# GEGLU feed-forward on one core: the head's transposing transfers of x move to ScalarE's queue in halves

## The chip, the cores and the metric

The kernel runs on one core of a Trainium2 chip. The metric is device time in microseconds (us), the median of three runs. The engines are called by the profile's short names: PE (TensorE matmul), PEld (TensorE weight load), DVE (VectorE), ACT (ScalarE), POOL (GpSimd), SP (SyncE). SP and ACT can each start DMA transfers on a queue of their own; "SPq" and "ACTq" are the times in which these two engines issue. A "transposing transfer" is a DMA that reads rows of x from DRAM and writes them transposed into SBUF.

## The reference

```python
B, S, D, F = 32, 32, 1024, 3584          # x is (1024 tokens) x 1024, bf16

def reference(x, w_gate, w_up, w_down):
    return (_gelu(x @ w_gate) * (x @ w_up)) @ w_down     # gelu: tanh approximation
```

The kernel does both big products by a scheme of Strassen's kind with seven products of half-size blocks. In the first stage x transposed is cut into four blocks of 512 model dimensions by 512 tokens, and the two weight matrices are treated as the other operand: for one 128-column strip of F, `a11` and `a12` are the upper and lower half of w_gate's rows, `a21` and `a22` those of w_up. `b11`, `b12` are the upper half of the model dimension for tokens 0 to 511 and 512 to 1023, `b21`, `b22` the lower half for the same tokens. Sums of weights (`s1` to `s4`) and of x blocks (`t1` to `t4`) enter the seven products.

## The kernel before

The work around the change is the head, the first 30 us. Its instructions are written out by hand in the order in which each engine is to run them (`tc.manual_schedule()`); a semaphore is put wherever one instruction needs another's result. Each engine runs its own list in order, so an instruction that waits holds everything behind it on that engine.

Every DMA signals its end on one of eight completion semaphores. They are given out in turn, and a DMA that comes eighth after another has to wait until that other one has landed before it is issued. The built instruction lists show these waits.

The head goes like this:

- The product `a12 b21` needs no sums, so it is computed ahead for 24 strips of 128 columns, in six groups of four (`group_ahead` and the loops before it, lines 326 to 340, 344 and 352). One strip is four matmuls (`k` = 0 to 3, one for each 128 rows of `b21`) into one bank of PSUM. Then ACT or DVE copies the bank to SBUF (`ahead`, lines 299 and 338), in groups 0 to 3 by turns (strips 0 and 2 of a group on ACT, 1 and 3 on DVE), in groups 4 and 5 on ACT alone.
- There are eight banks: six with the tag "A" and two with the tag "C", each handed out in turn. A strip can begin only when the copy that empties its bank has run. Groups use the tags CCAA, AAAA, CCAA, AAAA, AACC, CCAA.
- The first two 128-row pieces of `b21` don't come from a transposing transfer: the rows of x are loaded as they are (`x_nat`, two transfers, `load_nat`), transposed on PE through an identity matrix (line 264) and copied by DVE (line 267). The other two pieces, and the whole of `b11`, `b12` and `b22`, come by transposing transfers (`load_xT`, line 218): one of 256 KB for the rest of `b21`, and one of 512 KB each for the others, all four issued by SP.
- The columns of w_gate for the groups ahead come in `a12a` (groups 0 and 1) and `a12b` (groups 2 to 5) by `load_ahead` (line 211), the weights of the first chunks in `wu` and `wg` by `load_w` (line 135), nearly all issued by SP.
- DVE forms `t1 = b12 - b11` (line 345) and `t2 = b22 - t1` (351) between the adds of the first products (303), then `t3`, `s3` and `t4`; POOL forms the sums `s1`, `s2`, `s4` of chunk 0 from `wu`, `wg` and `a12a` as they land.
- ACT's list begins with three DMA issues: `probe` (line 207), a fetch of 128 bytes of w_gate that nothing reads, the second half of `x_nat`, and the first half of `a12a` of group 1. Then come the load of the activation table and the copies.

After the head the kernel loops over chunks of two strips, PE-bound, and then computes the second product from the stored gelu products.

Of the kernel before, what the change touches and what calls it, by code (L numbers as in the profile page):

```python
# [13 lines left out]
def kernel(  # L14
# [20 lines left out]
    nc = tc.nc  # L35
    P = nc.NUM_PARTITIONS
    fp32 = mybir.dt.float32
    f32r = mybir.dt.float32r
    bf16 = mybir.dt.bfloat16
# [9 lines left out]
    DT, FT = D // P, F // P  # L49
    KD = DT // 2  # L50
# [4 lines left out]
    KQ = DT // 4  # L55
# [8 lines left out]
    wg_r = w_gate.rearrange("(dt dp) f -> dp dt f", dp=P)  # L64
# [8 lines left out]
    xpool = one.enter_context(tc.tile_pool(name="x", bufs=1))  # L73
# [33 lines left out]
    def acc(tag):  # L107
        return ps1.tile([P, NB], fp32, name=f"ps{tag}", tag=tag, bufs=BANKS[tag])
# [28 lines left out]
    def load_w_all(ci, which):  # L137

        alloc_w(ci, which)
        if (ci, which) != (NCH - 1, 0):  # L140
            load_w(nc.sync, ci, which, 0, KD if which == 0 and a12_stays(ci) else DT)
            return


        for d0 in (0, KD):
            load_w(nc.sync, ci, which, d0, d0 + KD)
# [4 lines left out]
    def quads(ci, fl=None):  # L151
        cols = slice(None) if fl is None else slice(fl * P, (fl + 1) * P)
        wg, wu = w_tiles[ci, 0], w_tiles[ci, 1]
        a12 = wg[:, KD:, cols]
        if a12_stays(ci):
            i, j = divmod(chunks[ci][0], KB)
            a12 = a12_ahead[i][:, :, j * P : (j + FC) * P][:, :, cols]
        return wg[:, :KD, cols], a12, wu[:, :KD, cols], wu[:, KD:, cols]
# [3 lines left out]
    def sums(ci, *engs):  # L162

        a11, a12, a21, a22 = quads(ci)
        s1, s2, s4, s3 = (
            spool.tile([P, KD, FC * P], f32r, name=n, tag=n)[:, :, : len(chunks[ci]) * P]
            for n in ("s1", "s2", "s4", "s3")
        )
        s_tiles[ci] = (s1, s2, s3, s4)
        yield engs[0].tensor_tensor(s1, a21, a22, ADD)  # L170
        yield engs[1].tensor_tensor(s2, s1, a11, SUB)  # L171
        yield engs[2].tensor_tensor(s4, a12, s2, SUB)  # L172
        yield engs[3].tensor_tensor(s3, a11, a21, SUB)  # L173
# [17 lines left out]
    NB_P = NB // P  # L191
# [3 lines left out]
    with tc.manual_schedule():  # L195
        def load_nat(eng, dt, p0, p1):
            eng.dma_start(  # L197
                out=x_nat[:, p0:p1, dt * P : (dt + 1) * P],
                in_=xf[p0 * P : p1 * P, (KD + dt) * P : (KD + dt + 1) * P].rearrange("(b p) d -> p b d", p=P),
            )  # L200
# [1 line left out]
        assert KQ == 2  # L202
        load_nat(nc.sync, 0, 0, NB_P)


        probe = xpool.tile([P // 8, KQ, 2], bf16, name="probe")
        nc.scalar.dma_start(out=probe, in_=wg_r[::8, KD : KD + KQ, :2])

        def load_ahead(i, k0, k1, eng=nc.sync):
            f0 = i * KB  # L210
            eng.dma_start(
                out=a12_ahead[i][:, k0:k1, :],
                in_=wg_r[:, KD + k0 : KD + k1, f0 * P : (f0 + KB) * P],
            )

        def load_xT(nb, d0, d1):
            t = ((b11, b12), (b21, b22))[d0 // KD][nb]
            nc.sync.dma_start_transpose(
                out=t[:, d0 % KD : (d1 - 1) % KD + 1, :], in_=xf[nb * NB : (nb + 1) * NB, d0 * P : d1 * P]
            )  # L220

        load_ahead(0, 0, 1)
        load_nat(nc.scalar, 1, 0, NB_P)
        load_ahead(0, 1, 2)
        load_xT(0, KD + KQ, DT)
        load_ahead(1, 0, KQ, nc.scalar)
        a12_ahead += [spool.tile([P, KD, KB * P], bf16, name="a12b", tag=t) for t in ("s2", "s4", "s1", "s3")]
        for i in (0, 1):
            load_ahead(i, KQ, KD)
        def load_halves(i):  # L230
            for k in range(0, KD, KQ):
                load_ahead(i, k, k + KQ)

        load_halves(2)
        load_halves(3)
        for which in (1, 0):
            load_w_all(0, which)
        load_ahead(4, 0, KD)
        load_xT(0, 0, KD)
        load_xT(1, 0, KD)  # L240
        load_ahead(5, 0, KD)
        load_xT(1, KD, DT)
        for which in (1, 0):
            load_w_all(1, which)

        def gelu(src, tag, bufs):
            h = ework.tile([P, NB], bf16, name=tag, tag=tag, bufs=bufs)[:, : src.shape[-1]]
            nc.scalar.activation(h, src, ACT.Gelu_apprx_tanh)  # L248
            return h


        gelu(ident[:, :1], "h0", 6)

        warm_ps = acc("A")
        for _ in range(NWARM):
# [26 lines left out]
        def product_ahead(ps, i, j, k0=0, k1=KD, cols=slice(None)):  # L282
            for k in range(k0, k1):
                nc.tensor.matmul(  # L284
                    ps[:, cols],
                    lhsT=a12_ahead[i][:, k, j * P : (j + 1) * P],
                    rhs=b21[:, k, cols],
                    start=(k == 0 and not cols.start),
                    stop=(k == KD - 1),
                    skip_group_check=True,  # L290
                )

        def group_ahead(i, tags, copies=(nc.scalar.copy,), between=None):
            for j, tag in enumerate(tags):
                if between and 2 * j == KB:
                    between()
                ps = acc(tag)
                product_ahead(ps, i, j)
                copies[j % len(copies)](ahead_at[i * KB + j], ps)
# [35 lines left out]
        for i in (0, 1):  # L335
            for j in range(KB):
                product_ahead(ps[i][j], i, j, KQ)
                both[j % 2](ahead_at[i * KB + j], ps[i][j])
        group_ahead(2, "CCAA", both)
        group_ahead(3, "AAAA", both)  # L340
        chunk0 = sums(0, *[nc.gpsimd] * 3, nc.vector)
        for _ in range(3):
            next(chunk0)
# [275 lines left out]
```

## Time and profile before

| | us |
|---|---|
| time, median of 3 runs (lowest to highest) | 274.18 (273.29 to 275.09) |
| profiled execution: first to last instruction (span) | 272.0 |
| PE busy in it | 267.1 (98%) |
| DVE, ACT, POOL busy | 201.2, 116.1, 119.3 |
| first matmul of the groups ahead starts | 4.31 |
| first matmul that reads the transposed half of `b21` | 8.89 |
| SP's issues of the four transposing transfers | 1.34, 5.32, 1.67, 3.65 |

The profiled execution's own time is known only as its span; the median of the runs is 2.2 us above it, for what lies before the first and after the last instruction and for differences between executions.

How to read it: a timeline row gives the start, the length, the engine, the line, and the operation as output <- input, and in brackets how long the engine sat idle before it and what ended that. A DMA row on SPq or ACTq is the issue alone; how long a transfer takes to land is told in the DMA view, counted from the start of the issue. Buffer numbers are left out of names, so `b` stands for any of the four blocks and `t` for any of their sums.

### The profile page before, as it was taken

How to read it: one execution, taken by the hardware profiler on the slowest of the kernel's cores; microseconds unless marked ns; L12 is line 12 of the kernel's file. 1: busy time of each engine (PE TensorE's matmuls, PEld its weight loads, DVE VectorE, ACT ScalarE, POOL GpSimd, SP SyncE). 2: the span in 40 equal slices, each digit the busy share in tenths (PEclk: the TensorE clock that was granted, in tenths of full speed). 3: DMA queues.
4: the chain of work that ended last, by engine and by line, in shares of the span. 5: the costliest groups of instructions: out<-in, count | busy, mean ns of one | idle time of the engine just before them, and what ended most of it. 6: DMA issues, size and time to landing. Idle time of an engine off the chain costs nothing.

```text
span 272.0 us, 3399 instructions
## 1 busy us (share of the span) xinstructions
PE 267.1 (98%) x1199; PEld 193.4 (71%) x1212; DVE 201.2 (74%) x205; ACT 116.1 (43%) x189; POOL 119.3 (44%) x60
## 2 busy tenths in 40 slices
PE   8999999999999999999999999999999999999995
PEld 4444776886787688688688687764458888888884
DVE  1448998886976876876787458569999999997721
ACT  2335865545644643645636535434000307770000
POOL 1090099976995994994995978000000000000000
PEclk9999999999999999999999999999999999999999
DMA  7999130504505505415234290005981437855111
GB/s 174 323 227 281 39 99 17 158 25 130 154 2 154 154 4 154 128 27 157 69 88 118 50 319 17 0 2 182 356 273 60 158 112 253 276 187 174 54 61 58
DMA packets 56048, 35.86 MB, mean 132 GB/s; under 512 B 9824, under 2 KB 56032, under 8 KB 56032
## 3 DMA queue, kind: packets, MB, share of 16 engines
q1 hardware_dynamic: 52736, 33.17, 42.6%
q10 hardware_dynamic: 3296, 2.49, 2.9%
q8 instruction: 9, 0.15, 0.2%
q14 instruction: 7, 0.06, 0.1%
HBM read 31.72 MB, written 2.10 MB: 124 GB/s over the span
## 4 chain that ended last, share of the span: by engine, by line
PE 97%; DMA 1%; issue 0%; SPq 0%; DVE 0%
PE psA L273 38%; PE psA L425 24%; PE psC L273 19%; PE psC L425 7%; PE psA L284 5%; PE psC L284 3%; PE psC L588 1%; DMA a12a<-in_w_gate_dram 1%; SPq L197 0%; PE tp L264 0%; DVE o_last L589 0%
## 5 line engine op out<-in xcount | busy, mean ns | idle before, releaser
L273 PE MATMUL psA<-t,s 128*128 128x512 f32 x224 | 57.2, 397 | 0.0
L248 ACT ACTIVATE h<-c 128x512 bf16<-128x512 f32 x56 | 34.6, 631 | 41.6 <-DVE c L303 41.6
L273 PEld LDWEIGHTS psA<-t,s 128*128 128x128 f32 x224 | 42.1, 188 | 9.5
L170 POOL TENSOR_TENSOR s<-wu 128x1024 fp32r<-128x1024 bf16 x13 | 28.8, 2215 | 32.9 <-DMA wu<-in_w_up_dram 27.9
L171 POOL TENSOR_TENSOR s<-s,wg 128x1024 fp32r<-128x1024 f32 x14 | 31.7, 2263 | 15.0 <-DVE s L170 14.0
L173 POOL TENSOR_TENSOR s<-wg,wu 128x1024 fp32r<-128x1024 bf16 x13 | 28.4, 2188 | 0.0
L273 PE MATMUL psA<-b,wg 128*128 128x512 bf16 x119 | 27.8, 379 | 0.6
L273 PE MATMUL psA<-t,a22r 128*128 128x512 f32 x112 | 27.9, 391 | 0.0
L273 PE MATMUL psC<-t,s 128*128 128x512 f32 x112 | 27.9, 391 | 0.0
L273 PE MATMUL psC<-b22r,s 128*128 128x512 f32 x112 | 27.6, 389 | 0.0
L303 DVE TENSOR_TENSOR c<-sn,psA 128x512 f32<-128x512 f32 x32 | 21.8, 682 | 6.7 <-PE psA L273 5.7
L308 ACT COPY sn<-psC 128x512 f32<-128x512 f32 x28 | 16.4, 590 | 20.9 <-PE psC L273 15.2
L273 PEld LDWEIGHTS psC<-t,s 128*128 128x128 f32 x112 | 21.0, 188 | 4.5
L273 PEld LDWEIGHTS psA<-t,a22r 128*128 128x128 f32 x112 | 21.0, 188 | 4.5
L273 PEld LDWEIGHTS psC<-b22r,s 128*128 128x128 f32 x112 | 21.0, 188 | 4.4
L303 DVE TENSOR_TENSOR c<-sn,psC 128x512 f32<-128x512 f32 x28 | 19.2, 688 | 6.5 <-PE psC L273 6.5
L273 PEld LDWEIGHTS <-wg 128*128 128x128 bf16 x128 | 11.8, 98 | 15.3 <-issue 2.4
L172 POOL TENSOR_TENSOR s<-wg,s 128x1024 fp32r<-128x1024 bf16 x10 | 21.6, 2158 | 0.8
L402 DVE TENSOR_TENSOR lo<-c,h 128x512 bf16<-128x512 f32 x14 | 20.4, 1459 | 0.9
L308 ACT COPY sn<-psA 128x512 f32<-128x512 f32 x32 | 18.4, 592 | 6.1 <-PE psA L273 6.0
L303 DVE TENSOR_TENSOR c<-ahead,psA 128x512 f32<-128x512 f32 x24 | 16.4, 687 | 4.0 <-PE psA L273 2.4
L321 DVE TENSOR_TENSOR hi<-h,psA 128x512 bf16<-128x512 bf16 x14 | 9.6, 688 | 12.4 <-PE psA L273 12.4
(85 smaller groups left out, 381.0 us busy)
## 6 DMA issues: line engine op xcount, KB each, us to landing
wu<-in_w_up_dram SPq DMA_DIRECT2D x14, 512.0 KB, 4.0
wdb<-in_w_down_dram SPq DMA_DIRECT2D x12, 512.0 KB, 4.9
wg<-in_w_gate_dram SPq DMA_DIRECT2D x9, 512.0 KB, 5.2
wdb<-in_w_down_dram SPq DMA_DIRECT2D x12, 384.0 KB, 4.5
v<-in_w_down_dram SPq DMA_DIRECT2D x4, 512.0 KB, 6.4
out_dram<-o_sb ACTq DMA_DIRECT2D x15, 128.0 KB, 1.7
wg<-in_w_gate_dram SPq DMA_DIRECT2D x6, 256.0 KB, 4.6
v<-in_w_down_dram SPq DMA_DIRECT2D x4, 384.0 KB, 7.5
```

The source lines that it names most:

```text
L170: yield engs[0].tensor_tensor(s1, a21, a22, ADD)
L171: yield engs[1].tensor_tensor(s2, s1, a11, SUB)
L172: yield engs[2].tensor_tensor(s4, a12, s2, SUB)
L173: yield engs[3].tensor_tensor(s3, a11, a21, SUB)
L248: nc.scalar.activation(h, src, ACT.Gelu_apprx_tanh)
L273: nc.tensor.matmul(ps, lhsT=lhs[:, k, :], rhs=rhs[:, k, :], start=(start and k == 0), stop=(k == KD - 1), skip_group_check=True,)
L284: nc.tensor.matmul(ps[:, cols], lhsT=a12_ahead[i][:, k, j * P : (j + 1) * P], rhs=b21[:, k, cols], start=(k == 0 and not cols.start), stop ...
L303: tt(t, s, ps, ADD)
L308: nc.scalar.copy(t, ps)
L321: tt(g_of(ft)[:, :NB], h0, psa, MUL)
L402: tt(g_of(ft)[:, NB:], added(sn5[fl], psa[fl]), h1[fl], MUL)
L425: nc.tensor.matmul(banks[m], lhsT=lhs(k)[:, m * P : (m + 1) * P], rhs=rhs(k), start=(start and k == 0), stop=(k == HF - 1), skip_group_che ...
```

## The change

The fetch of `probe` is taken out. `load_nat` for the second half of `x_nat` and `load_ahead` for group 1 move from ACT's queue to SP's. `load_xT` issues on ACT's queue, and every block now comes in two transfers of 256 KB. Three of them (the rest of `b21`, then both halves of `b11`) stand in ACT's list behind the load of the activation table and a one-column gelu; the other four stand between the copies of groups 0 to 3: behind ACT's copies of group 0 the first half of `b12`, of group 1 the second half, of group 2 the first half of `b22`, of group 3 the second half. SP's list now holds nothing but plain loads.

```diff
-        probe = xpool.tile([P // 8, KQ, 2], bf16, name="probe")
-        nc.scalar.dma_start(out=probe, in_=wg_r[::8, KD : KD + KQ, :2])
 ...
         def load_xT(nb, d0, d1):
             t = ((b11, b12), (b21, b22))[d0 // KD][nb]
-            nc.sync.dma_start_transpose(
+            nc.scalar.dma_start_transpose(
                 out=t[:, d0 % KD : (d1 - 1) % KD + 1, :], in_=xf[nb * NB : (nb + 1) * NB, d0 * P : d1 * P]
             )

         load_ahead(0, 0, 1)
-        load_nat(nc.scalar, 1, 0, NB_P)
+        load_nat(nc.sync, 1, 0, NB_P)
         load_ahead(0, 1, 2)
-        load_xT(0, KD + KQ, DT)
-        load_ahead(1, 0, KQ, nc.scalar)
+        load_ahead(1, 0, KQ)
 ...
-        for i in (0, 1):
-            load_ahead(i, KQ, KD)
-        def load_halves(i):
-            for k in range(0, KD, KQ):
+        for i in range(4):
+            for k in range(KQ if i < 2 else 0, KD, KQ):
                 load_ahead(i, k, k + KQ)
-
-        load_halves(2)
-        load_halves(3)
         for which in (1, 0):
             load_w_all(0, which)
-        load_ahead(4, 0, KD)
-        load_xT(0, 0, KD)
-        load_xT(1, 0, KD)
-        load_ahead(5, 0, KD)
-        load_xT(1, KD, DT)
+        for i in (4, 5):
+            load_ahead(i, 0, KD)
         for which in (1, 0):
             load_w_all(1, which)
 ...
         gelu(ident[:, :1], "h0", 6)
+        load_xT(0, KD + KQ, DT)
+        load_xT(0, 0, KQ)
+        load_xT(0, KQ, KD)
 ...
                 both[j % 2](ahead_at[i * KB + j], ps[i][j])
+            load_xT(1, i * KQ, (i + 1) * KQ)
         group_ahead(2, "CCAA", both)
+        load_xT(1, KD, KD + KQ)
         group_ahead(3, "AAAA", both)
+        load_xT(1, KD + KQ, DT)
```

In the built instruction lists the eight completion semaphores now fall so that these transfers on ACT wait for others to land before they are issued: the half of `b21` for the first half of group 1's `a12a` (SP's fifth transfer), the first half of `b11` for the second half of group 0's `a12a`, its second half for the second half of group 2's `a12b`, the first half of `b12` for the first `wu`, its second half for the first `wg`, the first half of `b22` for group 4's `a12b`, and its second half for the second half of `b11`. In the kernel before, the half of `b21` waited for none.

## The prediction

> **What bounds the kernel now.** I read the page's busy line and its chain of waits first.
>
> ```profile
> PE 267.1 (98%) x1199; PEld 193.4 (71%) x1212; DVE 201.2 (74%) x205; ACT 116.1 (43%) x189; POOL 119.3 (44%) x60
> ...
> PE 97%; DMA 1%; issue 0%; SPq 0%; DVE 0%
> ```
>
> PE is busy 267.1 of 272.0 us and is 97% of the chain. So the head can gain only what PE idles there, and whatever makes PE wait there is paid in full at the end. Next, the timeline of the head:
>
> ```profile
> 2.32 1.34 SPq L218 DMA_TRANSPOSE b<-in_x_dram  x1
> ...
> 4.31 0.61 PE L284 MATMUL psC<-b,a12a 128*128 128x256 bf16 x2 [0.39 <-DMA a12a<-in_w_gate_dram]
> ...
> 6.88 0.47 SPq L135 DMA_DIRECT2D wu<-in_w_up_dram  x1
> ...
> 8.89 1.03 PE L284 MATMUL psC<-b,a12a 128*128 128x512 bf16 x4
> ...
> 10.30 6.99 SPq L218 DMA_TRANSPOSE b<-in_x_dram  x2
> ...
> 11.25 0.59 ACT L338 COPY ahead<-psA 128x512 f32<-128x512 f32 x1 [0.28 <-PE psA L284]
> ...
> 19.21 3.65 SPq L218 DMA_TRANSPOSE b<-in_x_dram  x1
> ...
> 21.29 2.29 DVE L345 TENSOR_TENSOR t<-b,b 128x2048 fp32r<-128x2048 bf16 x1 [1.14 <-DMA b<-in_x_dram]
> ...
> 24.43 1.89 PE L284 MATMUL psC<-b,a12b 128*128 128x512 bf16 x8
> ```
>
> PE waits 0.39 us for a12a before 4.31, and is then all but continuous. At 8.89 it first reads the transposed half of b21. SP pays 12 us for issuing four transposing transfers, but no PE row waits for that. DVE's 1.14 us wait for b12 costs nothing: t1 is done at 23.58 and PE first reads it at 27.70. The issues of that early window, with the time to landing, and the DMA rate by microsecond:
>
> ```profile
> a12a<-in_w_gate_dram ACTq DMA_DIRECT2D x1, 256.0 KB, 4.6
> a12a<-in_w_gate_dram SPq DMA_DIRECT2D x1, 128.0 KB, 4.4
> b<-in_x_dram SPq DMA_TRANSPOSE x1, 4.9
> ```
>
> ```profile
> 8.00:9.00 1.00, 1.00 (x6) 0.49 (x5) 0.00 (x0) 0.00 (x0) 0.00 (x0) 1.00 1.11 347
> ...
> 15.00:16.00 1.00, 1.00 (x6) 0.42 (x5) 0.00 (x0) 0.59 (x1) 0.92 (x2) 1.00 1.21 299
> 16.00:17.00 1.00, 1.00 (x6) 0.48 (x5) 0.69 (x1) 0.14 (x1) 1.00 (x1) 1.00 1.28 290
> ```
>
> The half of b21, issued at 2.32, landed at 7.2, 1.7 us before its use. The last column (GB/s) says that the transfers are limited by bandwidth: 347 with wide weight rows, 290 to 299 while mostly b11 is moved.
>
> **First matmuls: a gain of 0.2 us.** With probe and ACT's two loads gone from the other queue, group 0's first a12a has only x_nat's first half beside it. It landed at 4.27 (1.25 + 3.0); x_nat's own 2.5 us for the same 128 KB gives 3.75 at best. PE's transposes still follow the six warm-up matmuls (to 3.50) and the DVE copy that starts at 3.75 (0.29), so PE starts at about 4.1. x_nat's second half now lands after a12a's first piece, on one queue; it is needed at about 4.9 and landed at 4.4 before, so a slip of up to 0.5 us is hidden. I take -0.2, bounds -0.4 and +0.3.
>
> **The half of b21: +0.6 us.** Its issue now waits for SP's fifth transfer. SP issues at 0.74, 1.25 and on, 0.51 apart: the fifth at 2.78. Fastest, it lands after x_nat's 2.5, at 5.3; slowest when the same bytes landed before (1.73 + 4.6), at 6.3. Behind it come the issue and the transfer. Bounds: probe's 2.1 for nothing, plus 0.9 for a longer issue (1.34 against 0.45), plus 0.9 for 256 KB at 295 GB/s, is 3.9; b22, twice the size behind another load, took 5.7. So it lands between 9.2 and 12.0. I take 5.4 and 4.1, near the lower ends, because ACT's queue is empty then; that is 9.5. PE wants it at 8.7 (8.89 less the 0.2). PE stalls 0.8; net against before +0.6, bounds +0.3 and +3.1, or -0.2 if my lower bound on landing is too high by half a microsecond.
>
> **ACT's list: +1.2 us.** In groups 0 to 3 ACT empties half the banks, in 4 and 5 all. Behind each new transfer stand the copies of the next group, and PE waits for those. First half of b12: waits for wu. Before, wu was issued at 6.88 and landed 6.7 later, 13.6. Now both halves of b11 (512 KB) are asked for ahead of it or beside it: 1.8 us at 295 GB/s if all of it is in front, 15.4; none if SP's earlier issue makes up for it, 13.6. I take 14.7. One issue of a half took 1.34 on SP; ACT's plain issues took 0.49 and 0.53 against SP's 0.45 to 0.51, so 1.43. Then, by copies of 0.59:
>
> - issue to 16.1, group 1's two copies to 17.3
> - issue to 18.7, group 2's two to 19.9
> - issue to 21.3, group 3's two to 22.5
> - issue to 24.0, group 4's copies, 0.54 back to back: the third at 25.6
>
> Group 5's first strip uses the bank that this third copy empties; it started at 24.43, and now can't before 25.6. That is +1.2. Group 3's first strip (its copy started at 16.86, so it began a strip of 0.87 and a bit earlier, at 15.8) needs the copy that ends at 16.7 (+0.9), and so is inside. The three tasks that ACT no longer issues (0.45, 0.49, 0.53) only bring its table load forward, which no one waits for. Bounds: with wu at 13.6 and 1.34 an issue, -0.2, so nothing; with 15.4 and b22's 3.65 halved, 1.83, +3.5.
>
> **b22 and the sums of x: nothing.** Its second half is issued at 22.5 and at 4.9 lands at 27.4 (24.9 before). t2 then starts 2.2 us later than its 25.24 and ends at 29.7; PE read it at 29.74, plus what PE is late. Cover is about 1.2 us; if b22 is later than that, it adds one to one. b12, b11 and the a12b's for groups 4 and 5 come earlier or with more slack, since SP is free of 12 us of issuing.
>
> **Sum.** The waits lie one behind the other and the later absorbs the earlier: once PE is 0.6 late, ACT's chain costs only the rest. So the total is the greater, +1.2, and not 1.8. The span becomes 273.2; the runs' median lies 2.2 above the span, giving 275.4.
>
> **The skill against the trace.** The Trainium skill, "DMA: Bandwidth & Descriptors", section "Issuing engines are not separate DMA queues", says that transfers started from several engines share the same 16 DMA engines and that this saves only the time to issue. The rates above agree in that they stay below 352 whatever is queued; by the rule alone the change would be worth nothing, 274.2, as PE never waits for SP's issuing. The same page's "Latency and other measured facts" gives 261 GB/s for some transposing transfers; this trace shows 290 to 299, and the measurement decides. By 261, 512 KB would cost 0.2 us more, and the sum would be 275.6.
>
> **Rivals.**
>
> - *Hidden anyway.* ACT's chain fits between the groups (wu at 13.6, 1.34 an issue) and the half of b21 lands near 8.7. For: every wait involved has about 1 us of play. Against: both lower bounds must hold. Only the first gain is left: 274.0.
> - *The half of b21 comes late.* 6.3 plus 4.9 to 5.7 gives 11.2 to 12.0, +2.3 to +3.1: 276.5 to 277.3. For: SP's queue is full by then. The Trainium skill, "TensorE: Matmul & The Clock Gate", section on HAM oscillation, warns of idle gaps over 3.4 us; no wait here before shows one, and this would only just reach it.
> - *ACT is held in its issues as SP was, ending slower.* SP's 512 KB issues took 5.32 and 3.65 with much outstanding, 1.8 to 2.7 for a half. If ACT shares that limit with SP, an issue costs 2.2 and the four add 4 x 0.8 = 3.1 to the chain: +4.3, 278.5. It decides from 1.8 us an issue on, where the slowdown passes 1%. Against: ACT's queue itself holds little.
>
> **How the numbers follow.** Forecast (+0.4 to +2.2): 0.50. Hidden: 0.17. b21 late: 0.13. ACT held: 0.20. A difference within 1% (2.7 us) can't be told from no change here. Slower by more: most of "ACT held" (0.17), 0.05 of "b21 late", 0.07 from the forecast's upper tail, 0.29. Faster by more has no room, since PE idles too little: 0.03. The range is 273.8, just under "hidden", to 278.6, the price of "ACT held".
>
> **What would show it.** PE's wait before the first 512-wide matmuls of group 0, named b, about 0.8 us; the half of b21 landing near 9.5; ACT's issues near 1.4; wu landing near 14.7; PE's first matmul of group 5 near 25.6; after about 30 us the same intervals as before, all shifted. A wait of PE for t, or a different length of the chunks, would make me wrong in kind; issues of over 1.8 us, in size.

## The result and the profile after

| | before | after |
|---|---|---|
| time, median of 6 runs (lowest to highest), us | 274.05 (272.93 to 275.24) | 283.46 (281.58 to 284.05) |
| ratio after to before, 95% interval | | 1.0335 (1.0299 to 1.0371) |
| profiled execution: span, us | 272.0 | 282.0 |

The change makes the kernel 3.4% slower, not 0.4% as predicted, and the time lies outside the predicted range (273.8 to 278.6). The profiled execution of the changed kernel took 283.8 us, 1.8 more than its span.

The page of the changed kernel, its busy line, the granted clock in 40 slices, and the chain of work that ended last by engine and by line:

```profile
PE 269.8 (96%) x1212; PEld 193.6 (69%) x1212; DVE 202.1 (72%) x205; ACT 115.8 (41%) x189; POOL 119.6 (42%) x60
...
PEclk9959999999999999999999999999999999999999
...
PE 93%; DMA 5%; SPq 1%; DVE 0%; issue 0%
```

PE's share of the chain falls from 97% to 93%, and DMA's rises from 1% to 5%. Most of the work is as long as before: from 40 to 280 us PE is busy for 238.88 us, and in the kernel before, from 30 to 270 us, for 238.41. What is new lies in the third slice, where the granted clock is 0.5. The chain in order of time (start, length, what) names the two transfers:

```profile
2.77 4.25 DMA a12a<-in_w_gate_dram
7.04 9.30 DMA b<-in_x_dram
16.39 1.86 PE psC L276 x4
```

The first half of group 1's a12a takes 4.25 us and lands at 7.0. Only then can ACT issue the transposed half of b21, because of its completion semaphore, and this takes 9.30 us to land. The timeline of the head shows what waits:

```profile
4.09 0.38 PE L276 MATMUL psC<-b,a12a 128*128 128x256 bf16 x2 [0.17 <-DVE b L259]
...
7.04 8.55 ACTq L214 DMA_TRANSPOSE b<-in_x_dram  x3
7.07 1.90 PE L276 MATMUL psA<-b,a12a 128*128 128x512 bf16 x8 [0.73 <-DMA a12a<-in_w_gate_dram]
...
16.39 1.86 PE L276 MATMUL psC<-b,a12a 128*128 128x512 bf16 x4 [7.42 <-DMA b<-in_x_dram]
...
17.43 0.59 ACT L330 COPY ahead<-psC 128x512 f32<-128x512 f32 x1 [15.21 <-PE psC L276]
...
18.29 0.69 DVE L330 COPY ahead<-psC 128x512 f32<-128x512 f32 x1 [12.85 <-PE psC L276]
...
21.94 2.69 ACTq L214 DMA_TRANSPOSE b<-in_x_dram  x1
22.17 1.89 PE L276 MATMUL psC<-b,a12b 128*128 128x512 bf16 x8
...
29.88 2.28 DVE L340 TENSOR_TENSOR t<-b,b 128x2048 fp32r<-128x2048 bf16 x1
...
34.25 1.89 PE L276 MATMUL psC<-b,a12b 128*128 128x512 bf16 x8
```

PE starts 0.22 us earlier than before (4.09 for 4.31), waits 0.73 for a12a and then 7.42 for b. The 512-wide matmuls that read the transposed half start at 16.39; in the kernel before it was 8.89. That is 7.50 us late. Behind it the strips of group 0 come 0.86 apart, by their copies (17.43 and 18.29), where the kernel before had 0.44 (9.52 and 9.96). Stretches of 2 us show why (the columns: stretch, length, busy time of PE, PEld, DVE, ACT and POOL, then the granted clock, the DMA share and GB/s):

```profile
8.00:10.00 2.00, 0.97 (x5) 0.33 (x4) 0.00 (x0) 0.00 (x0) 0.00 (x0) 1.00 1.02 339
...
12.00:14.00 2.00, 0.00 (x0) 0.00 (x0) 0.00 (x0) 0.00 (x0) 0.24 (x1) 1.00 1.13 145
14.00:16.00 2.00, 0.00 (x0) 0.00 (x0) 0.00 (x0) 0.00 (x0) 1.87 (x1) 0.58 1.30 191
16.00:18.00 2.00, 1.61 (x4) 0.55 (x4) 0.00 (x0) 0.57 (x1) 1.50 (x1) 0.50 1.20 145
18.00:20.00 2.00, 2.00 (x6) 0.73 (x5) 0.70 (x2) 0.61 (x2) 1.92 (x2) 0.50 1.20 278
20.00:22.00 2.00, 2.00 (x8) 0.78 (x7) 1.18 (x2) 0.65 (x2) 0.84 (x1) 0.72 1.06 304
```

After PE's long wait the clock is 0.50 from 16 to 20 us and 0.72 on the mean from 20 to 22: six matmuls fit into 2 us where a full clock gives eleven. In the kernel before, group 2, which now starts at 22.17, started here:

```profile
12.35 1.89 PE L284 MATMUL psC<-b,a12b 128*128 128x512 bf16 x8
```

Two terms make up the loss:

- the waits, which make the first matmul on the transposed half 7.50 us late;
- the half clock: group 2 starts at 22.17 for 12.35, 9.82 late, so 9.82 - 7.50 = 2.32 us.

After that nothing more is lost. Group 5 starts at 34.25 for 24.43, again 9.82 late, and the span is 10.0 longer.

The same stretches have a second message. From 12 to 18 us the DMA engines are as busy as elsewhere (shares of 1.13 to 1.30) and move 145 to 191 GB/s. In the kernel before, the transposing transfers of b11 and b12 move from 15 us on, at 299 and 290 GB/s from 15 to 17, and then for one microsecond at less:

```profile
16.00:17.00 1.00, 1.00 (x6) 0.48 (x5) 0.69 (x1) 0.14 (x1) 1.00 (x1) 1.00 1.28 290
17.00:18.00 1.00, 1.00 (x7) 0.43 (x5) 0.27 (x1) 0.45 (x1) 1.00 (x1) 1.00 2.36 170
```

And the DMA view by queue tells how the 9.30 us are spent. From 7 to 11.2 us only packets of SP's queue move. The first packets of ACT's queue come between 11.2 and 11.4, when the last of SP's loads for group 3 (issued at 5.80, landed at 11.5) is nearly through. So some 4.2 us pass before the half begins to move, and some 5.1 us while it moves beside SP's next loads.

### The profile page after: what moved, and what is told of

The parts are those of the page before. It is cut to its first block, busy times and chain, and to the rows that moved or that the text cites. A ratio compares the mean times of both kernels' runs of the same rounds, so it can differ in the third digit from the quotient of the medians.

```text
span 282.0 us, 3417 instructions
## 1 busy us (share of the span) xinstructions
PE 269.8 (96%) x1212; PEld 193.6 (69%) x1212; DVE 202.1 (72%) x205; ACT 115.8 (41%) x189; POOL 119.6 (42%) x60
## 4 chain that ended last, share of the span: by engine, by line
PE 93%; DMA 5%; SPq 1%; DVE 0%; issue 0%
PE psA L265 37%; PE psA L420 23%; PE psC L265 18%; PE psC L420 7%; PE psA L276 5%; DMA b<-in_x_dram 3%; PE psC L276 2%; DMA a12a<-in_w_gate_dram 2%; PE psC L583 1%; SPq L207 0%; SPq L197 0%; DVE o_last L584 0%
## 5 line engine op out<-in xcount | busy, mean ns | idle before, releaser
L265 PE MATMUL psA<-b,wg 128*128 128x512 bf16 x128 | 29.4, 380 | 0.0
```

The costliest lines, as they stand in the source:

```text
L265: nc.tensor.matmul(ps, lhsT=lhs[:, k, :], rhs=rhs[:, k, :], start=(start and k == 0), stop=(k == KD - 1), skip_group_check=True,)
```

## The experiments

The questions were these. Is the 7.5 us the late issue of the transposed half, or its long way to landing? If the landing, is it that the transfer transposes, that it stands on another queue than SP's loads, or that so much is outstanding? And do ACT's long issues, which cost nothing in the changed kernel, cost something once the long wait is gone?

### The transposed half first in ACT's list

Edit, in the changed kernel: the half of b21 is ACT's first instruction and waits for nothing.

```diff
         load_ahead(0, 1, 2)
+        load_xT(0, KD + KQ, DT)
         load_ahead(1, 0, KQ)
 ...
-        load_xT(0, KD + KQ, DT)
         load_xT(0, 0, KQ)
```

> The changed kernel, but the half of b21 is ACT's first instruction, ahead of the table load, so that it is issued near 0.7 us and waits for no other transfer. Theory 'late issue': b21 was late only because it was issued at 7.04 instead of 2.32; then it lands by 6 us, PE's wait of 7.4 us and the half clock after it go, and the time is 274 to 275.5. Theory 'two queues': a transposing transfer on ACT's queue is slow beside a full SP queue whenever it is issued; then it lands after 9 us and the time stays above 277.

Measured: 278.82 us, ratio 1.0173 (1.0141 to 1.0206), span 277.5. Its timeline:

```profile
0.74 1.34 ACTq L214 DMA_TRANSPOSE b<-in_x_dram  x1
...
6.63 6.03 ACTq L214 DMA_TRANSPOSE b<-in_x_dram  x2
...
8.72 1.03 PE L275 MATMUL psC<-b,a12a 128*128 128x512 bf16 x4
...
12.71 0.59 ACT L329 COPY ahead<-psC 128x512 f32<-128x512 f32 x1 [9.10 <-PE psA L275]
...
13.35 1.89 PE L275 MATMUL psC<-b,a12b 128*128 128x512 bf16 x8 [1.01 <-ACT ahead L329]
...
20.58 1.24 ACTq L214 DMA_TRANSPOSE b<-in_x_dram  x1
...
22.99 3.45 PE L275 MATMUL psA<-b,a12b 128*128 128x512 bf16 x8 [2.58 <-ACT ahead L290]
...
29.73 1.89 PE L275 MATMUL psC<-b,a12b 128*128 128x512 bf16 x8
```

Issued at 0.74 the half lands 3.9 us later, and PE reads it at 8.72 without a wait. So the wait of 7.4 us is gone, but of the 10.0 us of span only 4.5 come back. Now the issues of b11's halves hold ACT: 6.03 us for two, so that ACT's first copy of group 0 comes at 12.71 instead of 9.52 and PE waits 1.01 us for the bank. The issue of b12's second half waits for an earlier transfer until 20.58, the copies behind it are late, and PE waits 2.58. The eight matmuls after that take 3.45 us instead of 1.89, in the profiled execution, whose mean clock is 0.994; in the other three it was 1.00. Group 5 is 5.3 us late. The waits for ACT are the rival "ACT is held in its issues", though held as much by a completion as by long issues; in the changed kernel they lay behind the 7.4 us.

### The transposed half back on SP's queue

Edit, in the changed kernel: this one half is issued by SP behind group 0's first a12a; the other six stay on ACT.

```diff
-        def load_xT(nb, d0, d1):
+        def load_xT(nb, d0, d1, eng=nc.scalar):
 ...
-            nc.scalar.dma_start_transpose(
+            eng.dma_start_transpose(
 ...
         load_ahead(0, 1, 2)
+        load_xT(0, KD + KQ, DT, nc.sync)
         load_ahead(1, 0, KQ)
 ...
-        load_xT(0, KD + KQ, DT)
         load_xT(0, 0, KQ)
```

> The changed kernel, but the half of b21 goes back to SP's queue at its old place (fifth there); the other six halves stay on ACT. Both theories: it lands near 7.3 us and PE doesn't wait at group 0. 'Late issue': what is left costs at most my chain of ACT's copies, so 274 to 275.5. 'Two queues': the halves of b11 then land late beside SP's loads (24 us in the changed kernel, wanted by PE at 22.7), so PE waits there by 1 to 3 us and the time is 275 to 278.

Measured: 281.71 us, ratio 1.0308 (1.0258 to 1.0357), span 279.8. The half is issued at 2.80 and lands 3.9 us later. PE's longest waits in the first 35 us, by what they are for (in total, times, longest):

```profile
PE psA L275 <- ACT ahead L290: 2.4, 1, 2.4
PE psA L275 <- DMA a12a<-in_w_gate_dram: 1.2, 1, 1.2
PE psC L275 <- ACT ahead L290: 1.2, 1, 1.2
```

Again no wait for b21, and again ACT's copies are late, here by issues of 5.63 us for two and then 1.24, 2.46, 3.49 and 4.03. After the wait of 2.36 us at 23.76 eight matmuls take 3.56 us. Group 5 is 7.5 us late. That is slower than either theory had it. Group 0's 512-wide matmuls start at 10.41, 1.5 us late, because of SP's loads; the other 6.0 us come with the six transfers that stay on ACT, which are thus enough for most of the loss.

### Keeping the clock up during the wait

Edit, in the changed kernel: 30 matmuls of zeros into a bank that is in use fill PE's wait.

```diff
+    zeros = xpool.tile([P, P], bf16, name="zeros")
+    nc.vector.memset(zeros, 0.0)
 ...
             product_ahead(ps[1][j], 1, j, 0, KQ)
+        for _ in range(30):
+            nc.tensor.matmul(ps[1][KB - 1], lhsT=zeros, rhs=ones_m, start=False, stop=False, skip_group_check=True)
```

> The changed kernel with 30 extra matmuls of zero weights (they add zero to a bank of group 1) in PE's list just before the wait for b21's half, 6.5 us of work inside a wait of 7.4 us. Theory 'clock': the matmuls after the wait ran at half speed because PE had idled; with the fill they run at 0.22 us and the time falls by 2.4, to 281. Rival: the half clock has another cause or the slow matmuls were fed late; then the time stays at 283.5.

Measured: 283.9 us, ratio 1.0377 (1.0333 to 1.0422), span 281.5. Two stretches, and two rows of the timeline:

```profile
16.00:18.00 2.00, 1.30 (x7) 0.58 (x7) 0.24 (x1) 0.59 (x1) 1.79 (x2) 1.00 1.21 144
18.00:20.00 2.00, 2.00 (x11) 0.94 (x10) 1.66 (x3) 0.59 (x1) 1.92 (x2) 1.00 1.12 283
```

```profile
21.95 5.37 ACTq L216 DMA_TRANSPOSE b<-in_x_dram  x1
...
28.49 1.89 PE L278 MATMUL psA<-b,a12b 128*128 128x512 bf16 x8 [1.26 <-ACT ahead L293]
```

The clock is 1.00 in both stretches and the strips are 0.43 apart again, so PE's idling was what brought the clock down. But the 2.3 us don't reach the end. Working sooner, PE meets the next wait: the issue of b12's second half takes ACT 5.37 us, its copies are late, and PE waits 1.26 us. Group 5 starts at 33.66 for 34.25, 0.6 us earlier; the span is 0.5 shorter and the median no different. Of the four executions the two with a mean clock of 1.00 took 283.2 and 283.3 us; the others, with 0.994 and 0.992, took 284.5 and 285.6.

### The plain loads alone

Edit, in the kernel before: no probe, x_nat's second half and group 1's first a12a issued by SP. All transposing transfers stay as they were.

```diff
-        probe = xpool.tile([P // 8, KQ, 2], bf16, name="probe")
-        nc.scalar.dma_start(out=probe, in_=wg_r[::8, KD : KD + KQ, :2])
 ...
-        load_nat(nc.scalar, 1, 0, NB_P)
+        load_nat(nc.sync, 1, 0, NB_P)
 ...
-        load_ahead(1, 0, KQ, nc.scalar)
+        load_ahead(1, 0, KQ)
```

> The kernel before with only the first part of the change: no probe, and x_nat's second half and group 1's first a12a on SP's queue; all transposing transfers stay on SP as before. My prediction's first step: PE starts 0.2 us earlier, nothing else moves, 274.0 (ratio 0.999). Rival: the loads that come behind one another on SP make PE wait in group 0 or 1, 274.5 to 275.5.

Measured: 275.33 us, ratio 1.0063 (1.0039 to 1.0088), span 273.1. PE's waits:

```profile
PE psA L282 <- DMA a12a<-in_w_gate_dram: 1.3, 1, 1.3
PE psC L282 <- DMA a12a<-in_w_gate_dram: 0.9, 1, 0.9
```

With every early load behind the other on one queue, PE waits twice for a12a. The 512-wide matmuls start at 9.86 instead of 8.89, and group 5 is as late, 0.97 us. So this part of the change costs about 1 us by itself, not -0.2. That it costs something rests on the times (the median is 1.7 us above that of the kernel before in the same round), since the early loads differ from one execution to the next: in the profiled execution of "Halves alone" below, whose list is that of the kernel before in this stretch, PE waits 1.62 us for a12a and the 512-wide matmuls start at 9.55.

### Without the probe alone

Edit, in the kernel before: the two lines of probe are taken out.

> The kernel before without the fetch of probe; nothing else. My prediction's first step: at most 0.2 us either way, ratio 0.999 to 1.001. Rival: the 1.7 us that the loads-only run lost belong to the missing first fetch, since its first a12a landed 0.3 us late; then the ratio is 1.003 to 1.006.

Measured: 273.77 us, ratio 0.9988 (0.9960 to 1.0016). The small fetch is worth nothing either way.

### Halves alone

Edit, in the kernel before: b11, b12 and b22 in two transfers each, still on SP.

```diff
-        load_xT(0, 0, KD)
-        load_xT(1, 0, KD)
+        for nb in (0, 1):
+            for k in (0, KQ):
+                load_xT(nb, k, k + KQ)
         load_ahead(5, 0, KD)
-        load_xT(1, KD, DT)
+        for k in (KD, KD + KQ):
+            load_xT(1, k, k + KQ)
```

> The kernel before, with b11, b12 and b22 fetched by halves, still from SP's queue and at the old places. 'Two queues' (transposing transfers on ACT's queue beside plain loads on SP's are what is slow): halving costs nothing that PE sees, 273.5 to 274.5. Rival 'halving': six short transposing transfers are themselves slower than three long ones; then DVE's sums of x come late and the time is over 275.

Measured: 273.83 us, ratio 0.9997 (0.9969 to 1.0025). Halves cost nothing, and on SP they land 4.0 to 6.4 us after their issue (median 4.7). In the changed kernel the seven halves took 9.3, 11.7, 10.8, 7.6, 6.3, 5.7 and 3.1, in the order of their issue. The size of the pieces isn't the cause.

### The same bytes on ACT's queue, not transposed

Edit, in the changed kernel: `load_xT` is a plain load of as many bytes, in the same place of ACT's list; the transposing is left out.

```diff
-            nc.scalar.dma_start_transpose(
-                out=t[:, d0 % KD : (d1 - 1) % KD + 1, :], in_=xf[nb * NB : (nb + 1) * NB, d0 * P : d1 * P]
+            nc.scalar.dma_start(
+                out=t[:, d0 % KD : (d1 - 1) % KD + 1, :].rearrange("p k (b d) -> p (k b) d", b=2),
+                in_=xf[nb * NB : (nb + 1) * NB, d0 * P : d1 * P].rearrange("(b p) d -> p b d", p=P),
```

> The changed kernel, but ACT's seven transfers are plain loads of the same bytes of x into the same tiles (512-byte rows), so nothing is transposed and the output is not the reference's. 'Transposing is slow beside loads on the other queue': as plain loads they land some 4.5 us after issue, b21's half near 11.5, PE waits 2 to 3 us, ACT's issues take 0.5 us, the time is 276 to 278. 'Any load on ACT's queue is held back behind a full SP queue': b21's half still lands after 14 us, 281 to 283.

Measured: 281.14 us, ratio 1.0254 (1.0185 to 1.0322), span 279.6. Its timeline, and three stretches:

```profile
7.09 2.50 ACTq L214 DMA_DIRECT2D b<-in_x_dram  x3
...
14.64 1.86 PE L277 MATMUL psC<-b,a12a 128*128 128x512 bf16 x4 [5.63 <-DMA b<-in_x_dram]
```

```profile
12.00:14.00 2.00, 0.00 (x0) 0.00 (x0) 0.00 (x0) 0.00 (x0) 0.00 (x0) 0.50 1.20 292
14.00:16.00 2.00, 1.36 (x4) 0.52 (x4) 0.00 (x0) 0.31 (x1) 1.18 (x1) 0.50 1.17 302
16.00:18.00 2.00, 2.00 (x6) 0.61 (x5) 0.69 (x1) 0.86 (x2) 1.92 (x2) 0.50 1.11 336
```

Most of the loss stays, as the second theory had it. Issued at 7.09 behind SP's loads, a plain 256 KB lands 7.5 us later, and PE waits 5.63. ACT's queue moves its first packets after 11.0 us here, much as in the changed kernel. So the 4 us before anything moves belong to what SP has outstanding, whatever the kind of the load. Transposing adds 1.8 us to this landing, nearly all of it behind the first packets. It also adds to the issues (three took 2.50 us here, 8.55 transposing), and it goes with the low rate: 292 to 336 GB/s here against 145 to 191.

### SP holds its loads until b11 has landed

Edit, in the kernel with the transposed half first: SP's later loads stand behind a fetch of a few bytes of b11.

```diff
+        for i in range(2):
+            load_ahead(i, KQ, KD)
 ...
         load_xT(0, 0, KQ)
         load_xT(0, KQ, KD)
+        hold = xpool.tile([P // 8, KQ, 2], bf16, name="hold")
+        nc.sync.dma_start(out=hold, in_=b11[: P // 8, 1 : 1 + KQ, :2])
 ...
```

> As the run with b21's half first on ACT, but SP issues nothing between group 1's a12a and the landing of both halves of b11: a fetch of a few bytes of b11 stands in SP's list as a hold. 'SP's backlog holds ACT': b11's halves, 3.0 us an issue beside a full SP queue, now take 1.3 each and land within 5.5 us of issue. Rival 'ACT's transposing issues are slow in themselves': still near 3.0 each. The time is no measure here, since group 2's weights come late by the hold: 276 to 281.

Measured: 281.35 us, ratio 1.0262 (1.0187 to 1.0336), which is no measure of the transfers, since the hold makes SP's loads late. What was to be read is the two issues of b11's halves and, in the DMA view of 5.0 to 6.6 us, their time to landing (the last number, a median):

```profile
5.05 2.97 ACTq L214 DMA_TRANSPOSE b<-in_x_dram  x2
...
10.14 0.75 SPq L237 DMA_DIRECT2D hold<-b  x1
```

```profile
b<-in_x_dram ACTq DMA_TRANSPOSE x2, 3.9
```

With SP held after its first few loads, two issues take 2.97 us instead of 6.03, and the halves land after 3.9 us instead of 8.8 and 12.6. Once SP resumes, behind 10.14, ACT's next transfers take 9.2 us and more. So without SP's list neither the landings nor these two issues of transposing transfers are long. The hold takes away both the loads that SP had issued earlier and those that it would have issued beside the halves, and this run doesn't tell the two apart.

### One transposing transfer on ACT, issued early

Edit, in the kernel before: no probe, and only the half of b21 moves to ACT, right behind x_nat's second half. This was to be the version that keeps what is good in the change.

```diff
         load_nat(nc.scalar, 1, 0, NB_P)
+        load_xT(0, KD + KQ, DT, nc.scalar)
         load_ahead(0, 1, 2)
-        load_xT(0, KD + KQ, DT)
```

> The kernel before, with one transposing transfer alone on ACT's queue: b21's half, issued near 1.2 us behind x_nat's second half, with no probe; all else on SP as before. 'Order of issue over both queues' (a transfer gets the DMA engines after what either queue has issued earlier): little is outstanding then, it lands by 6 us, ACT's issue takes 1.3 us and no copy waits behind it; 273 to 274.3, ratio 0.996 to 1.001. Rival 'ACT's queue is slow for transposing whenever SP loads': it lands after 8.9 us and PE waits, over 275.

Measured: 276.69 us, ratio 1.0095 (1.0059 to 1.0131), span 274.9. Its timeline, and two stretches of 1 us:

```profile
1.27 1.33 ACTq L216 DMA_TRANSPOSE b<-in_x_dram  x1
...
7.24 0.41 PE L282 MATMUL psC<-b,a12a 128*128 128x256 bf16 x2 [1.39 <-DMA a12a<-in_w_gate_dram]
...
8.30 3.56 PE L282 MATMUL psA<-b,a12a 128*128 128x256 bf16 x10
...
11.70 1.03 PE L282 MATMUL psC<-b,a12a 128*128 128x512 bf16 x4
```

```profile
4.00:5.00 1.00, 0.64 (x7) 0.39 (x5) 0.49 (x2) 0.75 (x2) 0.00 (x0) 1.00 1.05 174
...
8.00:9.00 1.00, 0.93 (x5) 0.33 (x3) 0.00 (x0) 0.00 (x0) 0.00 (x0) 0.50 1.11 351
```

The half lands in time, 6.2 us after its issue, at 7.5 (later than the first theory had it, earlier than the rival). But the transfers of SP beside it pay: a piece of group 0's a12a takes 5.4 us to land instead of 4.4, the rate falls to 174 GB/s from 4 to 5 us, and PE waits 1.39 us. The clock then falls to 0.50, and the 512-wide matmuls start at 11.70, 2.81 late; group 5 is 2.81 late too. The half clock isn't needed for the loss: five of the seven executions have a mean clock of 1.00 and took 275.7 to 277.4 us. None of the versions beats the kernel before.

Moving b12 and b22 alone to ACT, with b11 on SP, wasn't tried.

## Why the prediction was wrong, by its steps

**The half of b21: the step that failed.** It was to be issued at 5.4 and land 4.1 later, for a stall of 0.8 us. It was issued at 7.04 and landed 9.3 later, for a wait of 7.42. The issue lay outside the step's bounds because a12a landed at 7.0 (5.3 to 6.3 were given). The greater error is the term "to landing", bounded by 3.9 and 5.7. Its rows were of transfers with little outstanding, and "ACT's queue is empty then" was taken for an empty road. The trace of before held the row that should have been the upper end, a transposing transfer of b11 (512 KB), issued at 10.30 with SP's list outstanding (the DMA view from 10.2 to 10.4 us; the last number is the time to landing):

```profile
b<-in_x_dram SPq DMA_TRANSPOSE x1, 9.2
```

By that, even at the predicted 5.4, the half would have landed at 14.6, 5.9 us after its use at 8.7. In the changed kernel the half's 9.3 us were 4.2 before its first packet and 5.1 from there to landing; the lower bound, near which the prediction stayed, held 0.9 for moving 256 KB at 295 GB/s and 3.0 for all else. The plain loads on ACT and SP's hold show what lies behind both: a transfer waits for loads issued before it, also when they stand on the other queue, and then shares the DMA engines with what SP issues next.

**The clock: a missing term of 2.3 us.** The prediction named the rule of the Trainium skill, "TensorE: Matmul & The Clock Gate", section "HAM oscillation — how this bites in real kernels", that idle gaps of over about 3.4 us bring the clock down, and gave it no price, since no wait it foresaw was that long (3.1 us at the most). The wait of 7.4 us agrees with the rule. But waits of 2.36 and 2.58 us were followed by eight matmuls in 3.56 and 3.45 us, and one of 1.39 in the last experiment by a clock of 0.50; here the measurement decides, and shorter waits can cost too. They don't always: in the profiled executions the other waits of 1.0 to 1.7 us, eight of them, are followed by matmuls at full pace (those of 1.18, 1.26, 1.32 and 1.62 us, for instance).

**First matmuls: half right.** PE started at 4.09, as predicted (about 4.1), though single executions differ by more than the 0.2 us (with the same plain loads on SP it was 4.67 in "The plain loads alone"). But the loads that now stand behind one another on SP make PE wait for a12a: 0.73 us in the changed kernel, and alone 0.97 us to the end. The step looked at the first piece only.

**ACT's list: right in kind, hidden by the larger wait.** The chain was priced at +1.2 us, with issues of 1.43. They took 1.5 to 4.0 each (the first three 8.55 together, later ones 1.55, 2.69, 2.21 and 1.53, a mean of 2.0 for the four that the chain counted). This is near the rival "ACT is held in its issues as SP was" (2.2 each, 278.5), but in the changed kernel it cost nothing, since PE was already 9.8 late. The chain also began with b12 and left out the two issues of b11's halves, which stand before ACT's first copy: with the half of b21 first on ACT they took 6.03 us. ACT's chain decided only with the long wait gone: with the half of b21 first on ACT, or on SP, PE waited up to 2.6 us for ACT's copies, and group 5 was 5.3 and 7.5 us late.

**The sum as the greater, not the total: right.** Filling the clock's 2.3 us gained 0.5 of span, because ACT's chain took over. The half clock itself is no such term: it comes behind the wait and adds to it.

**b22 and the sums of x: right, but hardly tested.** t1 starts at 29.88, and no wait of PE for t appears. b22's second half landed at 31.5 for the predicted 27.4, 4.1 us later, more than the cover of 1.2 us; it cost nothing because PE was 9.8 us late by then. **Probe and halves: right.** Each is worth nothing measurable.

**The rivals.** "The half of b21 comes late" had the right mechanism and place, at 2.3 to 3.1 us instead of 7.5 + 2.3. "Hidden anyway" is excluded.

**The rule on queues.** The prediction weighed the Trainium skill, "DMA: Bandwidth & Descriptors", section "Issuing engines are not separate DMA queues", which says that issuing from several engines saves only the time to issue. The runs agree that a second queue is no second road. They differ in the price: here the second queue lost time, 0.95% with one transfer moved and 3.4% with all.

## What to carry to other kernels

A transfer's time to landing belongs to what is outstanding when it is issued, on any queue: take its bound from the slowest row of the trace with as much outstanding, not from the row of its kind with the least. Before moving an issue to an idle engine, ask when its completion semaphore lets it go and which copies stand behind it there. And where a PE-bound kernel comes to wait, add the half clock after the wait to the sum: here each of the five profiled waits of 2.29 to 7.42 us had it behind it, and of nine waits of 1.0 to 1.7 us one had.

## What the runs showed of the hardware

Three things were not expected.

- Transposing transfers on ACT's queue beside plain loads on SP's move fewer bytes at the same busy share: 145 to 191 GB/s from 12 to 18 us in the changed kernel and 172 and 189 from 14 to 18 with the half first on ACT, against 292 to 336 with plain loads on both. ACT's queue alone isn't slow: while SP was held, the transposing transfers had the DMA engines to themselves from 8.0 to 9.5 us and moved 253 to 272 GB/s. The kernel before also has one microsecond (17 to 18) at 170 on SP alone, so the mix of queues isn't the only way to a low rate. Why the mix is slow no run shows.
- Order across queues: 256 KB on ACT landed after 7.5 us (plain) or 9.3 (transposing) when issued at 7.1 behind SP's list, with no packet moved for the first 4 us, and after 3.9 when issued at 0.74 or while SP was held. The order isn't strict: in the last experiment SP's piece of a12a, issued at 1.76, landed at 7.2, before the half issued at 1.27 on ACT.
- ACT's time to issue a transposing half varies: 1.34 us at the start, two in 2.97 with SP held, two in 6.03 without, and 5.37 for one at the most. Three plain issues in the same place took 2.50. It isn't set by SP's outstanding loads alone, since single issues of 1.24 us stand beside a full list of SP too (at 15.87 with the half back on SP, at 20.58 with it first on ACT). Which limit holds the issuing engine isn't shown.
